# One order of steps replaced by another in a hand-scheduled kernel of block-sparse attention, Fourier mixing and an MLP

## The chip, the cores and the metric

The kernel runs on one core of a Trainium2 chip. The metric is the device time of one execution in microseconds (us). A core has five engines that work beside each other, each through its own list of instructions in order: TensorE (PE in the profile; its weight loads are PEld), VectorE (DVE), ScalarE (ACT), GpSimd (POOL) and SyncE (SP), which here only issues DMAs. An instruction whose input or whose buffer isn't ready makes its engine wait, and all that stands behind it in that engine's list waits too.

## The reference

Queries, keys and values have 4 batches, 8 heads, 768 positions and 64 channels. Keys are averaged over blocks of 64 positions; each query keeps its own block and those among the 3 best of the 12 blocks by a gate score, and attends causally within them. The heads are put side by side into `x` (768 x 512 a batch), which is mixed by a two-dimensional Fourier transform and sent through an MLP with a residual:

```python
    k_rep = k.reshape(B, H, n_blocks, block, D).mean(axis=3)
    gate_scores = np.einsum('bhsd,bhnd->bhsn', q, k_rep)
...
    top_idx = np.argsort(gate_scores, axis=-1)[..., -top_k:]
...
    mask = mask & (pos[:, None] >= pos[None, :])
    scores = np.where(mask, scores, -1000000000.0)
...
    return np.matmul(attn, v).astype(np.float32)
...
    X = np.fft.fft(x, axis=1)
    X = np.fft.fft(X, axis=2)
    mixed = np.real(X).astype(np.float32)
    u = x + mixed
    mu = np.mean(u, axis=-1, keepdims=True)
    var = np.mean((u - mu) ** 2, axis=-1, keepdims=True)
    un = (u - mu) / np.sqrt(var + 1e-06)
    ch = np.maximum(un @ w_ch1, 0.0) @ w_ch2
    return (u + ch).astype(np.float32)
```

## The kernel before

The work is cut into 16 pairs of heads, P = 0 to 15, four to a batch b. Every piece of work is a step with a short name and its indices, and the string `ORDER` lists all steps of the program in one sequence. A loop at the end of the kernel calls them in that sequence (lines 765 to 769), inside a context that leaves the instructions of each engine in the order in which they were called. So the string fixes five lists, one for each engine. What an engine waits for follows from the data: the framework adds a wait wherever an instruction reads what another engine writes, overwrites what another still reads, or shares a PSUM tile with another engine.

The steps, in the order in which a pair and then a batch passes through them:

- Loads, issued by SP: `Lq`, `Lk`, `Lv` (lines 263 to 283). `Li` loads a constant. `W` and `X` load the weights of the MLP, issued by POOL.
- Preparing a pair: `tk`, `tq` turn keys and queries on PE in early pairs; later pairs are turned on VectorE by `kb` and `qc`. `ks`, `kh` make block sums on VectorE, `kc` copies the keys on ScalarE, `qs` copies the queries on POOL.
- The gate: `g` on PE, then `gt`, `gx`, `gl`, `gm` on VectorE; from pair 7 on, `K` writes the mask into the query buffer with eight copies on POOL (line 400).
- Scores: `s:P,i` on PE, six tiles i = 0 to 5 (line 410), `e:P,i` the exponential on ScalarE, `d:P,i` the causal select on POOL for the part on the diagonal. `vc` converts the values on POOL. `v` multiplies the exponentials of a pair with its values (42 matmuls, PE), and needs all six `d` and `vc`; `x` divides by the sums on VectorE.
- Fourier transform of a batch: `fs`, `fd`, `f` fold `x` by symmetry on VectorE. `pg` is a small read on POOL that stands ahead of the reuse of a buffer. `y:b,0` and `y:b,1` are the first transform on PE, `ty` (ScalarE) and `tr` (VectorE) copy its result in two ways, `m:b,0` to `m:b,2` are the second transform on PE.
- Sum and normalization: `u` (VectorE) adds `x`, `xu` (ScalarE) scales the sum, and `un` turns it for the MLP, for batch 0 on PE and VectorE (`xt`, `un`), for batches 1 to 3 by two DMA transposes on SP for each `un` (line 605). `bn`, `nv` (VectorE) and `nr` (POOL) make the reciprocal deviation.
- MLP: `w:b,it`, it = 0 to 15, is the first product, 8 matmuls on PE that need all three `un` of the batch; `r` is its relu, on ScalarE, for every fourth on VectorE. `c:b,st,h` is the half h of the second product for the 128 rows st, 8 matmuls; two neighbouring st share one PSUM tile. `o` scales and adds the residual on VectorE, `od` stores the rows (SP). In the last batch the rows st = 5 are cut into two halves of the columns instead, each with 16 matmuls (`c:3,5,0` and `c:3,5,1`, `o:3,5` and `o:3,6`).

All PSUM tiles of the kernel come from one pool of four tiles of two banks each: score tiles, gate tiles, `v`, `y`, `m`, `w` and `c` share them. A `c` tile is held from its first half product until both of its `o`. The exponentials have two buffers, so the first `e` of a pair needs the `v` of an earlier one to be done; `u` has five buffers, so some `u` need a store of an earlier batch to have landed.

Of the kernel before, what the change touches and what calls it, by code (L numbers as in the profile page):

```python
# [173 lines left out]
r:3,11 nv:3 c:3,5,0 c:3,5,1 c:3,0,0 nr:3 pg:3 c:3,1,0 c:3,0,1 c:3,1,1 o:3,0 c:3,2,0 c:3,2,1 o:3,5
c:3,4,0 c:3,4,1 o:3,6 c:3,3,0 o:3,1 o:3,2 o:3,4 c:3,3,1 o:3,3 od:3,1 od:3,5 od:2,5 od:2,2 od:3,0
od:2,4 od:2,3 od:3,2 od:3,6 od:3,4 od:3,3
"""
assert PT_W == 5376 and len(COL) == 42

# [620 lines left out]
```

## Time and profile before

| | us |
|---|---|
| median of 3 executions | 294.94 |
| lowest and highest | 294.92 and 302.59 |
| the profiled execution | 294.79 |
| its span, from first to last instruction | 292.8 |

The span is the profile's own time and lies 2.0 us below the device time of that execution. In the profile, L668 is a line of the source, and an operand pair such as `c<-w_sb,hT` names the tile written and the tiles read. The lines that matter here: `sc` L421 and L426 are the steps `s`, `pt` L443 `e`, `pt` L449 `d`, `av` L461 `v`, `yp` L531 and L537 `y`, `mx` L564 and L565 `m`, `u` L578 `u`, `x` L590 `xu`, `h` L641 and L643 `w`, `hT` L651 and L653 `r`, `c` L660 and L668 `c`, `u` L680 `o`. L221 and L224 are helpers that many steps on VectorE and POOL share.

A matmul's own duration contains the time that it takes to run through the pipeline, in which the next one already runs. What a step costs TensorE is therefore read from a run of many of its matmuls, not from the duration of one.

### The profile page before, as it was taken

To read this page: it belongs to the slowest core of one execution; us is meant where nothing else is said; L and a number is where in the kernel's file an instruction comes from. 1 tells how busy PE (TensorE), PEld (TensorE's weight loads), DVE (VectorE), ACT (ScalarE), POOL (GpSimd) and SP (SyncE) were. 2 spreads that over 40 slices of the span, in tenths; PEclk is the share of its full clock that TensorE was granted. 3 is DMA by queue.
4 is the path that set the end of the run, shared out by engine and by line. 5 is a ranking of instruction groups with operands and counts; after the bars stand their busy time and mean duration, and the time that the engine had idled before them with its cause. 6 is when DMAs were issued, how large, how long until landed. Compare 5 with 4: busy or idle time off the path is not lost.

```text
span 292.8 us, 6583 instructions
## 1 busy us (share of the span) xinstructions
PE 276.4 (94%) x2537; PEld 169.1 (58%) x2537; DVE 198.3 (68%) x604; ACT 164.1 (56%) x205; POOL 113.2 (39%) x286
## 2 busy tenths in 40 slices
PE   7799999899999999989999999999999998999993
PEld 4466777655556456635665466556655644657441
DVE  2999999989875998969758858862672457212022
ACT  3698989866686437579858463776242240534000
POOL 2267527406689598400790483438000000003000
PEclk9999999999999999999999999999999999999999
DMA  9999999999999968376700021930000332000063
GB/s 201 268 222 238 198 206 196 202 175 161 158 209 167 192 126 171 66 144 178 112 2 1 0 85 42 128 108 0 2 2 0 143 67 44 0 2 0 2 233 125
DMA packets 118287, 33.52 MB, mean 114 GB/s; under 512 B 111024, under 2 KB 115056, under 8 KB 118256
## 3 DMA queue, kind: packets, MB, share of 16 engines
q1 hardware_dynamic: 112592, 28.47, 45.6%
q0 software_dynamic: 3664, 4.19, 9.0%
q10 hardware_dynamic: 2000, 0.44, 0.7%
q8 instruction: 20, 0.33, 0.5%
q14 instruction: 11, 0.09, 0.1%
HBM read 28.63 MB, written 6.29 MB: 119 GB/s over the span
## 4 chain that ended last, share of the span: by engine, by line
PE 63%; DVE 16%; ACT 8%; SPq 6%; DMA 3%; issue 2%; POOL 0%; DVEq 0%; ACTq 0%; POOLq 0%
PE c L668 21%; PE h L641 15%; PE h L643 8%; ACT pt L443 5%; SPq L277 5%; PE sc L426 5%; PE av L461 4%; DVE kr L306 2%; PE yp L531 2%; DVE u L680 2%; DVE q L328 2%; DMA nat<-in_q_dram 1%; PE warmps L705 1%; DVE u L578 1%; PE c L660 1%
## 5 line engine op out<-in xcount | busy, mean ns | idle before, releaser
L443 ACT ACTIVATE pt<-sc 128x1024 f16<-128x1024 f32 (+1 forms) x96 | 83.0, 923 | 27.6 <-PE sc L426 22.9
L668 PE MATMUL c<-w_sb,hT 128*128 128x512 f16 x368 | 83.8, 379 | 2.6 <-DVE u L680 2.6
L641 PE MATMUL h<-unT,w 128*128 128x512 f16 x256 | 84.7, 380 | 0.6 <-DVE unT L602 0.2
L643 PE MATMUL h<-unT,w 128*128 128x256 f16 x256 | 69.8, 273 | 0.0
L653 ACT ACTIVATE hT<-h 128x768 f16<-128x768 f32 x48 | 37.4, 809 | 42.9 <-PE h L643 42.7
L668 PEld LDWEIGHTS <-hT 128*128 128x128 f16 x368 | 35.4, 98 | 42.0 <-issue 3.3
L449 POOL TENSOR_SCALAR_AFFINE_SELECT pt<-pt 128x256 f16<-128x256 f16 x96 | 37.2, 413 | 48.8 <-ACT pt L443 32.5
L641 PEld LDWEIGHTS <-w 128*128 128x128 f16 x256 | 25.0, 98 | 29.6 <-issue 0.9
L680 DVE SCALAR_TENSOR_TENSOR u<-c,rs,u 128x512 f32<-128x512 f32 (+1 forms) x25 | 17.3, 720 | 35.3 <-PE c L668 31.8
L224 POOL TENSOR_SCALAR_AFFINE_SELECT qk<-mt 32x160 f16<-32x160 f16 x72 | 23.6, 348 | 16.5 <-DVE mt L398 14.9
L643 PEld LDWEIGHTS <-w 128*128 128x128 f16 x256 | 25.0, 98 | 5.3 <-issue 1.4
L426 PE MATMUL sc<-qk 96*128 96x128 f16 (+3 forms) x144 | 26.8, 306 | 1.2 <-ACT pt L443 1.2
L221 POOL TENSOR_TENSOR t<-vr,rs 128x6 f32<-128x6 f32 x12 | 2.4, 198 | 63.8 <-DVE rs L621 63.2
L651 DVE TENSOR_SCALAR hT<-h 128x768 f16<-128x768 f32 x16 | 15.1, 951 | 17.3 <-PE h L643 17.1
L224 POOL TENSOR_SCALAR_AFFINE_SELECT qk<-q 64x768 f16<-64x768 f32 (+1 forms) x25 | 20.8, 831 | 15.5 <-DVE q L328 11.0
L461 PE MATMUL av<-v,pt 128*128 128x65 f16 x672 | 23.1, 194 | 1.0 <-DVE u L578 1.0
L461 PEld LDWEIGHTS <-pt 128*128 128x128 f16 x672 | 22.2, 97 | 3.2 <-POOL qk L224 0.8
L590 ACT ACTIVATE x<-u,nm 128x512 f16<-128x512 f32 x24 | 15.8, 715 | 12.6 <-DVE nm L584 12.3
L426 PEld LDWEIGHTS <-qk 96*128 96x128 f16 x144 | 13.1, 98 | 10.7 <-issue 1.6
L578 DVE SCALAR_TENSOR_TENSOR u<-mx,x 128x512 f32<-128x512 f32 x24 | 15.6, 685 | 4.3 <-PE mx L565 2.5
L610 DVE BATCH_NORM_STATS2 bst<-u 128x6 f32<-128x512 f32 x24 | 16.1, 670 | 0.0
L421 PE MATMUL sc<-qk 64*128 64x512 f16 (+3 forms) x112 | 14.6, 306 | 1.5 <-ACT pt L443 0.8
(99 smaller groups left out, 353.4 us busy)
## 6 DMA issues: line engine op xcount, KB each, us to landing
nat<-in_v_dram SPq DMA_DIRECT2D x16, 384.0 KB, 5.0
out_dram<-u SPq DMA_DIRECT2D x23, 256.0 KB, 2.3
nat<-in_q_dram SPq DMA_DIRECT2D x36, 96.0 KB, 3.0
nat<-in_k_dram SPq DMA_DIRECT2D x17, 192.0 KB, 3.6
nat<-in_k_dram SPq DMA_DIRECT2D x28, 96.0 KB, 2.9
nat<-in_q_dram SPq DMA_DIRECT2D x13, 192.0 KB, 3.6
w_sb<-in_moe_w_ch_dram POOLq DMA_DIRECT2D x2, 1024.0 KB, 10.0
w<-in_moe_w_ch_dram POOLq DMA_DIRECT2D x2, 768.0 KB, 9.3
```

What stands on the lines that cost most here:

```text
L224: nc.gpsimd.affine_select(out=out, in_=in_, pattern=[[0, i] for i in n], base=0, channel_multiplier=0, compare_op=ALU.is_ge, fill=0.0)
L426: nc.tensor.matmul(ps[:, e, co:co + q1 - q0], qk[0:96, e, 1, 128 * jt:128 * jt + 128], qk[0:96, e, 0, q0:q1], start=True, stop=True)
L443: nc.scalar.activation(out=d["pt"][:, o:o + 2 * n].rearrange("p (e c) -> p e c", e=2), in_=d["sc", i][:, :, 0:n], func=AF.Exp, scale=0.125)
L449: nc.gpsimd.affine_select(out=dg, in_=dg, pattern=[[0, 2], [1, 128]], base=0, channel_multiplier=-1, compare_op=ALU.is_ge, fill=0.0)
L461: nc.tensor.matmul(av[:, e, 66 * st:66 * st + 65], pt[:, co:co + 128], vv[:, e, jt, 0:65], start=(cnt == 0), stop=(cnt == 20))
L578: nc.vector.scalar_tensor_tensor(out=u_b[:, k2, :].rearrange("p (m two) -> p two m", two=2), in0=mps[:, k2, :].rearrange("p (two m) -> p t ...
L610: nc.vector.bn_stats(out=bst, in_=u_t[b, kt // 2][:, kt % 2, :])
L641: nc.tensor.matmul(hp[:, 0:512], w1s, unT[:, dt, 0:512], start=(dt == 0), stop=(dt == NDT - 1))
L643: nc.tensor.matmul(hp[:, 512:768], w1s, unT[:, dt, 512:768], start=(dt == 0), stop=(dt == NDT - 1))
L653: nc.scalar.activation(out=hT, in_=hp, func=AF.Relu)
L668: nc.tensor.matmul(c_ps[b, g[0]][:, st - g[0], :], h_t[b, it][:, 128 * st:128 * (st + 1)], w2_sb[:, it, :], start=(it == 0), stop=(it == N ...
L680: nc.vector.scalar_tensor_tensor(out=o, in0=ps, scalar=st_t[b][1][:, st:st + 1], in1=o, op0=ALU.mult, op1=ALU.add)
```

## The change

The string `ORDER` is the same up to `w:0,4` in the middle of the first MLP product of batch 0, and another one from there to its end. Both hold the same steps, each once; nothing else in the kernel differs. Each PSUM tile's reads and writes stand in the string in an order that every engine keeps. These lines are the first of the diff and the last:

```diff
-r:0,12 w:0,7 r:0,7 s:6,5 s:6,2 w:0,13 r:0,13 e:6,5 w:0,10 w:0,4 w:0,3 e:6,2 qc:10 gx:8 kb:10 ks:10
-kh:10 qc:9 d:6,1 d:6,4 d:6,0 qs:7 K:7 vc:5 d:6,2 X:0 d:5,3 Li:0 Lv:7 Lq:12 Lv:8 Lv:9 s:7,5 r:0,3
...
-r:3,11 nv:3 c:3,5,0 c:3,5,1 c:3,0,0 nr:3 pg:3 c:3,1,0 c:3,0,1 c:3,1,1 o:3,0 c:3,2,0 c:3,2,1 o:3,5
-c:3,4,0 c:3,4,1 o:3,6 c:3,3,0 o:3,1 o:3,2 o:3,4 c:3,3,1 o:3,3 od:3,1 od:3,5 od:2,5 od:2,2 od:3,0
+r:0,12 w:0,7 r:0,7 s:6,5 s:6,2 w:0,13 r:0,13 e:6,5 w:0,10 w:0,4 d:5,3 vc:5 qs:7 d:6,4 K:7 X:0 Li:0
+Lv:7 Lq:12 Lv:8 Lv:9 qc:9 gx:8 gl:8,0 gl:8,1 gm:8 kb:10 kh:9 bn:0,5 v:5 s:7,5 e:6,2 g:9 gt:9 s:7,0
...
+pg:3 nr:3 r:3,13 w:3,15 r:3,15 c:3,5,1 c:3,4,1 c:3,0,0 c:3,2,1 o:3,4 o:3,6 c:3,0,1 o:3,2 o:3,0
+c:3,3,1 o:3,3 c:3,1,0 c:3,1,1 c:3,5,0 o:3,1 o:3,5 od:3,6 od:2,3 od:2,2 od:2,4 od:3,4 od:3,2 od:3,0
```

Read for single engines, the parts of the two lists that the prediction speaks of are these. TensorE, from the parting to the first MLP product of batch 1, old and new:

```
old: w:0,3 s:7,5 v:5 s:7,0 w:0,14 g:9 g:10 w:0,8 s:7,4 w:0,15 s:7,3 s:7,1 w:0,11 s:7,2 w:0,9 v:6
     s:8,4 s:8,3 c:0,2,0 c:0,3,0 s:8,1 v:7 c:0,0,0 s:8,0 s:9,2 c:0,1,0 s:9,4 c:0,3,1 s:8,5 c:0,1,1
     s:9,3 s:9,5 c:0,2,1 c:0,0,1 y:1,1 g:11 y:1,0 s:9,0 s:8,2 c:0,4,0 s:9,1 m:1,1 m:1,0 m:1,2 v:8
     v:9 c:0,5,0 c:0,5,1 s:11,5 s:11,1 s:10,1 c:0,4,1 s:10,0 g:12 s:11,0 s:10,4 s:11,3 w:1,1
new: v:5 s:7,5 g:9 s:7,0 s:7,3 w:0,8 s:7,4 w:0,3 s:7,1 s:7,2 s:8,3 w:0,9 w:0,14 w:0,11 v:6 s:8,5
     w:0,15 g:10 c:0,0,0 s:9,1 v:7 s:8,4 c:0,1,0 s:8,2 c:0,2,0 s:8,1 s:8,0 c:0,0,1 s:9,5 c:0,1,1
     y:1,1 y:1,0 c:0,3,0 m:1,0 m:1,1 c:0,4,0 s:9,3 c:0,3,1 s:9,4 s:9,0 c:0,2,1 m:1,2 c:0,5,0 g:11
     c:0,5,1 s:9,2 v:8 s:10,5 c:0,4,1 s:10,3 s:10,0 v:9 s:10,2 s:11,0 w:1,0
```

TensorE, from the second transform of batch 2, and of batch 3, to the first `w` of the batch:

```
old: m:2,2 m:2,0 m:2,1 c:1,4,1 v:12 c:1,2,0 c:1,5,1 s:14,3 c:1,3,0 s:14,0 s:14,4 v:13 s:15,3 c:1,3,1
     s:15,0 s:14,5 s:15,5 c:1,2,1 s:14,2 w:2,3
new: m:2,0 c:1,5,1 s:15,1 s:15,4 m:2,1 s:15,0 v:13 c:1,2,0 s:14,4 m:2,2 c:1,2,1 s:14,5 s:14,1 s:14,2
     c:1,3,0 c:1,3,1 s:15,5 s:14,0 s:15,2 w:2,4
old: m:3,1 m:3,0 c:2,5,0 m:3,2 c:2,2,0 c:2,2,1 c:2,4,1 c:2,5,1 c:2,3,0 c:2,3,1 w:3,15
new: m:3,1 m:3,0 c:2,0,0 c:2,1,0 w:2,10 c:2,4,0 c:2,1,1 c:2,0,1 c:2,4,1 c:2,2,0 c:2,3,0 m:3,2 c:2,5,0
     c:2,2,1 c:2,3,1 c:2,5,1 w:3,14
```

POOL from the parting on, and SP around the transposes:

```
POOL old: d:6,1 d:6,4 d:6,0 qs:7 K:7 vc:5 d:6,2 X:0 d:5,3 d:7,5 d:7,0 vc:6 vc:7 K:8 qs:9 d:6,5 d:6,3
          d:7,4 X:1 d:7,1 d:7,2 d:7,3 vc:8 K:9 vc:9 nr:0
POOL new: d:5,3 vc:5 qs:7 d:6,4 K:7 X:0 qs:9 K:8 d:7,3 d:6,3 d:6,2 d:6,5 d:6,0 d:7,4 vc:6 d:7,2 d:6,1
          d:7,5 X:1 qs:10 K:9 vc:7 d:7,0 d:7,1 nr:0
SP old:   Lq:13 od:0,1 Lq:14 od:0,2 od:0,0 Lk:12 Lk:13 un:1,1 un:1,0 un:1,2 Lk:14
SP new:   Lq:13 od:0,1 od:0,0 Lq:14 Lk:12 un:1,1 un:1,2 un:1,0 od:0,3 Lk:13 Lk:14
SP old:   od:1,1 od:1,0 Lv:14 un:2,2 Lv:15 un:2,1 un:2,0 od:1,3 od:1,5 od:2,0 od:1,2 od:2,1 od:1,4
          un:3,0 un:3,2 un:3,1
SP new:   Lv:14 Lv:15 od:1,1 od:1,0 un:2,1 un:2,0 un:2,2 od:1,3 od:1,2 od:1,5 od:1,4 un:3,1 un:3,0
          od:2,1 od:2,0 un:3,2
```

VectorE around the sums of batch 1, and at the end:

```
old: tr:1,0 qc:12 gx:11 gl:11,0 gl:11,1 gm:11 u:1,1 u:1,0 u:1,2 x:8 kb:12 x:9
new: tr:1,0 u:1,1 gl:10,0 u:1,0 bn:1,3 gl:10,1 kb:11 ks:11 kh:11 gm:10 qc:12 o:0,2 u:1,2 gt:11 gx:11
     o:0,3 gl:11,0 bn:1,0 gl:11,1 gm:11 x:8
old: u:3,0 u:3,1 u:3,2 bn:3,2 o:2,5 o:2,2 ... o:3,0 o:3,5 o:3,6 o:3,1 o:3,2 o:3,4 o:3,3
new: u:3,1 o:2,0 o:2,1 bn:3,2 bn:3,3 u:3,2 o:2,4 o:2,2 ... o:3,4 o:3,6 o:3,2 o:3,0 o:3,3 o:3,1 o:3,5
```

More of the change, by code (lines that the diff above doesn't have):

```diff
@@ new lines @@
+fs:7,1 fd:7,1 fs:4,0 fd:6,0 qc:11 fd:7,0 fd:6,1 f:1,1 f:1,0 f:1,2 f:1,3 y:1,1 e:9,1 e:8,4 e:8,2
+e:8,1 e:8,0 e:9,5 o:0,0 o:0,1 ty:1,1 y:1,0 c:0,3,0 tr:1,1 ty:1,0 m:1,0 tr:1,0 m:1,1 c:0,4,0 s:9,3
+c:0,3,1 s:9,4 s:9,0 c:0,2,1 e:9,3 u:1,1 gl:10,0 m:1,2 xu:1,1 e:9,0 c:0,5,0 u:1,0 bn:1,3 Lv:10 Lv:11
+Lk:11 Lq:13 od:0,1 od:0,0 Lq:14 Lk:12 gl:10,1 kb:11 ks:11 kh:11 gm:10 qc:12 g:11 c:0,5,1 o:0,2 e:9,4
+kc:10 u:1,2 kc:11 xu:1,2 gt:11 gx:11 s:9,2 o:0,3 gl:11,0 xu:1,0 e:9,2 bn:1,0 gl:11,1 gm:11 d:8,2
+vc:8 vc:9 d:8,3 d:8,1 d:8,4 d:9,5 qs:11 d:8,5 d:9,1 d:9,3 d:9,4 d:8,0 d:9,0 vc:10 K:10 qs:12 d:9,2
@@ new lines @@
+pg:1 K:11 vc:11 v:8 s:10,5 c:0,4,1 s:10,3 s:10,0 x:8 o:0,4 o:0,5 kb:12 ks:12 kh:12 v:9 s:10,2 s:11,0
+un:1,1 un:1,2 un:1,0 od:0,3 Lk:13 Lk:14 od:0,5 Lv:12 od:0,4 Lv:13 Lk:15 Lq:15 od:0,2 w:1,0 x:9 g:12
+s:11,2 s:11,4 e:10,5 s:10,4 w:1,12 e:10,3 gt:12 e:10,0 w:1,10 s:11,1 e:10,2 e:11,0 s:11,5 w:1,1
+r:1,0 e:11,2 s:10,1 kb:13 ks:13 gx:12 gl:12,0 fs:9,1 gl:12,1 gm:12 kb:14 qc:13 kh:13 fs:9,0 fs:8,0
+w:1,8 e:10,4 e:11,4 w:1,11 r:1,12 r:1,11 r:1,10 e:11,5 r:1,1 s:11,3 e:10,1 w:1,6 qc:14 ks:14 kh:14
@@ new lines @@
+w:1,15 w:1,13 r:1,8 kc:13 g:14 e:11,3 g:13 e:11,1 r:1,15 gt:13 r:1,6 gx:13 bn:1,4 gl:13,0 gl:13,1
+w:1,5 gm:13 d:11,5 d:10,5 d:10,1 d:10,4 d:10,2 d:11,4 K:12 d:11,3 d:10,3 d:11,2 d:11,0 d:10,0 K:13
+d:11,1 qs:13 qs:14 v:10 gt:14 w:1,4 r:1,5 gx:14 x:10 gl:14,0 fs:10,0 bn:1,1 w:1,2 w:1,7 r:1,4 kc:12
+v:11 r:1,7 r:1,13 x:11 fs:11,0 qc:15 r:1,2 w:1,3 r:1,3 s:12,0 kc:14 e:12,0 s:13,3 w:1,9 s:12,4
+s:13,5 w:1,14 s:13,2 e:13,3 r:1,9 e:13,5 c:1,0,0 gl:14,1 gm:14 kb:15 fs:10,1 bn:1,5 ks:15 kh:15
+r:1,14 e:12,4 s:12,2 g:15 bn:1,2 nv:1 gt:15 s:12,5 c:1,1,0 s:13,4 e:13,2 s:12,1 e:12,2 e:12,1
@@ new lines @@
+c:1,0,1 s:12,3 e:12,5 e:13,4 s:13,0 e:12,3 s:13,1 kc:15 e:13,1 c:1,1,1 c:1,4,0 e:13,0 gx:15 fs:8,1
+fs:11,1 fd:11,1 gl:15,0 fd:10,0 fd:11,0 fd:10,1 f:2,1 f:2,2 gl:15,1 gm:15 f:2,0 f:2,3 nr:1 d:12,0
+d:12,1 d:13,3 d:13,2 d:13,5 d:12,3 qs:15 d:12,5 d:12,4 d:12,2 vc:12 d:13,0 K:15 K:14 pg:2 d:13,1
+d:13,4 vc:13 y:2,0 v:12 c:1,4,1 ty:2,0 y:2,1 o:1,0 s:15,3 tr:2,0 c:1,5,0 ty:2,1 m:2,0 c:1,5,1 o:1,1
+x:12 s:15,1 s:15,4 fs:12,0 tr:2,1 e:15,3 m:2,1 e:15,1 s:15,0 e:15,4 v:13 u:2,0 xu:2,0 c:1,2,0 o:1,4
+s:14,4 o:1,5 m:2,2 u:2,1 xu:2,1 c:1,2,1 x:13 s:14,5 bn:2,3 e:15,0 e:14,4 u:2,2 fs:13,1 fs:13,0
@@ new lines @@
+bn:2,1 s:14,1 s:14,2 c:1,3,0 c:1,3,1 bn:2,0 bn:2,4 bn:2,5 bn:2,2 nv:2 e:14,5 o:1,2 s:15,5 o:1,3
+xu:2,2 Lv:14 Lv:15 od:1,1 od:1,0 un:2,1 un:2,0 un:2,2 od:1,3 od:1,2 od:1,5 od:1,4 s:14,0 e:14,1
+e:14,2 e:15,5 e:14,0 s:15,2 w:2,4 r:2,4 e:15,2 s:14,3 w:2,8 r:2,8 w:2,7 e:14,3 w:2,3 r:2,3 r:2,7
+w:2,14 d:14,4 d:15,0 d:14,2 d:14,5 d:15,4 d:15,3 nr:2 d:15,2 d:15,5 d:15,1 vc:15 d:14,3 d:14,1
+d:14,0 vc:14 v:15 w:2,13 w:2,11 r:2,13 v:14 r:2,11 w:2,6 r:2,14 w:2,0 w:2,9 w:2,2 w:2,5 r:2,9 r:2,2
+r:2,0 r:2,5 x:15 w:2,1 x:14 r:2,1 fs:14,0 fs:15,0 fs:15,1 fs:12,1 fd:15,1 fs:14,1 fd:14,0 fd:14,1
@@ new lines @@
+fd:15,0 f:3,2 f:3,1 f:3,3 f:3,0 y:3,1 ty:3,1 y:3,0 tr:3,0 r:2,6 w:2,15 ty:3,0 w:2,12 r:2,12 tr:3,1
+m:3,1 m:3,0 c:2,0,0 u:3,0 c:2,1,0 w:2,10 r:2,15 c:2,4,0 r:2,10 c:2,1,1 c:2,0,1 u:3,1 c:2,4,1 c:2,2,0
+c:2,3,0 o:2,0 m:3,2 o:2,1 c:2,5,0 bn:3,2 bn:3,3 u:3,2 c:2,2,1 xu:3,1 xu:3,0 xu:3,2 un:3,1 un:3,0
+od:2,1 od:2,0 un:3,2 o:2,4 c:2,3,1 c:2,5,1 o:2,2 bn:3,0 w:3,14 w:3,0 w:3,1 r:3,0 w:3,3 r:3,14 w:3,12
+bn:3,5 o:2,3 r:3,12 w:3,7 w:3,4 bn:3,1 w:3,5 r:3,5 w:3,2 r:3,3 r:3,1 w:3,6 r:3,6 w:3,11 r:3,2 r:3,4
@@ L177 @@
+w:3,10 o:2,5 r:3,7 w:3,9 r:3,9 c:3,2,0 c:3,3,0 w:3,8 c:3,4,0 r:3,8 r:3,10 r:3,11 w:3,13 bn:3,4 nv:3
+pg:3 nr:3 r:3,13 w:3,15 r:3,15 c:3,5,1 c:3,4,1 c:3,0,0 c:3,2,1 o:3,4 o:3,6 c:3,0,1 o:3,2 o:3,0
+c:3,3,1 o:3,3 c:3,1,0 c:3,1,1 c:3,5,0 o:3,1 o:3,5 od:3,6 od:2,3 od:2,2 od:2,4 od:3,4 od:3,2 od:3,0
+od:3,3 od:2,5 od:3,1 od:3,5
 """
```

46 lines of the change are left out of this document (5 added, 41 removed).

## The prediction

> **What bounds the kernel now.** First the head of the page and its busy time by engine.
>
> ```profile
> span 292.8 us, 6583 instructions
> ## 1 busy us (share of the span) xinstructions
> PE 276.4 (94%) x2537; PEld 169.1 (58%) x2537; DVE 198.3 (68%) x604; ACT 164.1 (56%) x205; POOL 113.2 (39%) x286
> ```
>
> TensorE is the candidate. A mean over the span doesn't say where it stands idle, so next I read the busy time by stretch, from the point at which the two lists part. The first two columns are the stretch and its length, then come busy time and instructions of PE, PEld, DVE, ACT and POOL, then the granted clock.
>
> ```profile
> 74.60:115.00 40.40, 39.69 (x362) 23.88 (x360) 32.79 (x105) 24.68 (x30) 32.76 (x73) 1.00 0.98 172
> 115.00:130.00 15.00, 12.57 (x148) 7.69 (x146) 12.52 (x34) 9.17 (x13) 5.34 (x15) 1.00 0.54 96
> 130.00:230.00 100.00, 99.85 (x837) 60.92 (x835) 66.60 (x193) 59.57 (x74) 37.45 (x103) 1.00 0.27 58
> 230.00:245.00 15.00, 13.44 (x73) 6.97 (x73) 8.81 (x25) 4.00 (x6) 0.00 (x0) 1.00 0.36 89
> 245.00:285.00 40.00, 40.00 (x234) 22.78 (x233) 9.97 (x19) 9.07 (x12) 2.50 (x13) 1.00 0.11 42
> 285.00:292.80 7.80, 2.95 (x13) 1.07 (x11) 2.16 (x3) 0.00 (x0) 0.00 (x0) 0.95 0.34 124
> 206.60:218.30 11.70, 11.70 (x78) 7.04 (x75) 7.98 (x17) 3.24 (x4) 0.00 (x0) 1.00 0.01 1
> ```
>
> PE is full from 130 to 230 and from 245 to 285, at clock 1.00. Where it isn't full, it misses 40.40 - 39.69 = 0.71, 2.43, 0.15 and 1.56 us in the first, second, third and fourth stretch. Of the 4.85 us in the sixth, part is a stall and the rest is the time behind the last product. The PE timeline of two of these stretches names the stalls (in brackets: idle time, and who ended it).
>
> ```profile
> 117.06 1.44 PE L461 MATMUL av<-v,pt 128*128 128x65 f16 x42 [0.52 <-DVE u L578]
> 119.03 1.45 PE L461 MATMUL av<-v,pt 128*128 128x65 f16 x42 [0.52 <-DVE u L578]
> ```
>
> ```profile
> 242.62 3.62 PE L668 MATMUL c<-w_sb,hT 128*128 128x512 f16 x16 [1.50 <-DVE u L680]
> ```
>
> Last the timeline of all engines at the end.
>
> ```profile
> 286.10 1.41 DVE L680 SCALAR_TENSOR_TENSOR u<-c,rs,u 128x512 f32<-128x512 f32 x2 [6.34 <-PE c L668]
> 286.88 3.06 SPq L685 DMA_DIRECT2D out_dram<-u  x4
> 286.90 1.89 PE L668 MATMUL c<-w_sb,hT 128*128 128x512 f16 x8 [0.84 <-DVE u L680]
> ```
>
> PE ends at 286.90 + 1.89 = 288.79; the last result step and store take the other 4.01 us. So behind the cut TensorE has 0.71 + 2.43 + 0.15 + 1.56 + 0.84 = 5.69 us of stalls. The change adds and removes no instruction, so PE's work is the same before and after. The time moves by two things alone: the sum of these stalls, and what lies behind PE's last product. That caps the gain at 5.7 us and what the end gives; the loss has no such cap.
>
> **The prices.** From the chain of waits, which cuts TensorE's stream into pieces without overlap:
>
> ```profile
> 71.98 0.38 PE h L641
> ...
> 159.78 3.45 PE c L668 x16
> 163.24 0.86 PE sc L426 x4
> ...
> 187.07 1.28 PE av L461 x42
> ```
>
> Half a column sum `c` (8 matmuls) is 1.73 us, a score tile `s` 0.43 (the small tile `s:P,5` about 0.1, an estimate by its columns), a pair's `v` 1.28. The last row of the table by stretch holds nine whole products `w` in 11.70 us: 1.30 each. `w:0,10` starts at 71.98 and `w:0,4` is the last step that both lists share on PE, so the new order begins there at about 71.98 + 2 x 1.30 = 74.6. `m` has half the columns of a half `c`: 0.87, an estimate.
>
> For the other engines, the groups of POOL, VectorE and ScalarE (count | busy, mean ns of one | idle before):
>
> ```profile
> L449 POOL TENSOR_SCALAR_AFFINE_SELECT pt<-pt 128x256 f16<-128x256 f16 x96 | 37.2, 413 | 48.8 <-ACT pt L443 32.5 <-issue 9.0 <-PE c L668 6.7
> L224 POOL TENSOR_SCALAR_AFFINE_SELECT qk<-mt 32x160 f16<-32x160 f16 x72 | 23.6, 348 | 16.5 <-DVE mt L398 14.9
> L224 POOL TENSOR_SCALAR_AFFINE_SELECT qk<-q 64x768 f16<-64x768 f32 x18 | 15.0, 833 | 4.5 <-DVE q L326 3.2 <-PE sc L426 0.7
> L224 POOL TENSOR_SCALAR_AFFINE_SELECT v<-nat 128x768 f16<-128x768 f32 x16 | 14.5, 914 | 0.2
> ```
>
> ```profile
> L680 DVE SCALAR_TENSOR_TENSOR u<-c,rs,u 128x512 f32<-128x512 f32 x23 | 16.6, 742 | 35.3 <-PE c L668 31.8 <-POOL rs L221 3.5
> L610 DVE BATCH_NORM_STATS2 bst<-u 128x6 f32<-128x512 f32 x24 | 16.1, 670 | 0.0
> L578 DVE SCALAR_TENSOR_TENSOR u<-mx,x 128x512 f32<-128x512 f32 x24 | 15.6, 685 | 4.3 <-PE mx L565 2.5 <-DMA out_dram<-u 1.7
> ...
> L326 DVE STREAM_TRANSPOSE q<-nat 128x768 f32<-128x768 f32 x9 | 8.7, 967 | 0.0
> ```
>
> ```profile
> L590 ACT ACTIVATE x<-u,nm 128x512 f16<-128x512 f32 x24 | 15.8, 715 | 12.6 <-DVE nm L584 12.3
> ```
>
> And the transposes that SP issues (line 605), and the stores:
>
> ```profile
> L605 SPq DMA_TRANSPOSE unT<-x x18: 1189/1220/2121, 118.5 to 242.5; - x18
> ...
> DMA to landing us min/median/max: 2.4/2.5/5.2
> ```
>
> ```profile
> out_dram<-u SPq DMA_DIRECT2D x23, 256.0 KB, 2.3
> ...
> out_dram<-u SPq DMA_DIRECT2D x2, 128.0 KB, 2.0
> ```
>
> **The change part by part.** *POOL's new order up to the first `v`.* POOL now takes `d:5,3`, `vc:5` and `qs:7` first, whose inputs are long there, and defers the selects of pair 6. From `K:7` to the last step that `v:7` needs, `d:7,1`, its list holds three `K` of about 8 x 0.348 + 0.3 = 3.1, two `qs` of 1.7, two `vc` of 0.91, eleven `d` at about 0.4 and two weight loads that I take at 0.9 each: 9.3 + 3.4 + 1.8 + 4.4 + 1.8 = 20.7 us. `K:7` waits for a VectorE step that isn't moved and starts near 70.5, so `v:7` can start near 91.2. On PE there stand ahead of `v:7`, from 74.6: `v:5`, `v:6` (2.6), seven full and two small `s` (3.2), `g:9`, `g:10` (0.9, an estimate), six `w` (7.8), one `c` (1.7): 16.2, that is 90.8. Stall about 0.4 (0 to 1.5), where the old order misses 0.71 in its stretch.
>
> *First chain (batch 1, where 2.43 us are lost now).* The new list does three halves `c` fewer before `y:1,1` and keeps them for the chain. Behind `m:1,1` PE has, up to `w:1,0`: six halves `c` (10.4), `m:1,2` (0.9), eight full and one small `s` (3.5), two `v` (2.6), `g:11` (0.4): 17.8. The chain meanwhile needs `u:1,1` and `u:1,0` (2 x 0.685 and a short step, 1.5 each), then on VectorE what stands ahead of `u:1,2`: `bn` (0.9 with its second instruction), `kb:11`, `ks:11`, `qc:12` (about 0.97 each), `o:0,2` (0.74) and short steps (0.6), 5.1 together; `u:1,2` 1.5; `xu:1,2` 2 x 0.715 = 1.4; two transposes for `un:1,2` (2.4), one more (1.2) and the landing of the last (2.5): 17.1. Cover and need are even. I take 0.5 for handovers; the bounds are 0 and, with the slowest landing of 5.2, about 2.5.
>
> *Second chain (batch 2, nearly hidden now).* The new list places `m:2,2` late. Behind it stand three halves `c` (5.2), four full and two small `s` (1.9): 7.1. Need: `u:2,2` 1.5, `xu:2,2` 1.4, a transpose 1.2, landing 2.5: 6.6. Again even: 0.5 (0 to 2.5), where the old order loses at most 0.15.
>
> *Third chain (batch 3, 1.56 lost now).* In the old order `o:2,5` stands ahead of `o:2,2` on VectorE and waits for `c:2,5,1`, and PE's `c:2,3,0` waits for `o:2,2`: the 1.50 of the row. The new order finishes `c:2,3,0` before any `o` of that tile, so this stall goes. What is late next is `un:3,2`: behind `m:3,2` only four halves `c` are left (6.9) against 1.5 + 1.4 + 1.2 + 2.5 = 6.6. I take 0.5 (0 to 2.5).
>
> *The end.* Now `o:3,2` waits 6.34 us for PE although its half of the tile was summed long before, and `c:3,3,1`, which writes the other half, waits 0.84 for `o:3,2`. In the new list another half `c` stands between each `o` and the next access to its tile (1.73 against 0.74), so the 0.84 goes. The last product is the half-width `c:3,5,0`, its `o` about 0.37 (half of 0.742, an estimate) instead of 0.742, its store 2.0 instead of 2.3: 0.67 less behind PE's end.
>
> The Trainium skill, PSUM — Partial Sum Buffer, section PSUM bank collisions raise a hardware error, asks that engines be kept apart by bank and quadrant only; the two halves of this tile are two banks, so by it `c:3,3,1` need not have waited. The trace differs: the program does wait, 0.84 us, so it orders whole tiles. By the page the end would give 0.67 alone and the sum would come out 0.8 us higher, near 291.9.
>
> *Sum.* Stalls of 5.69 go; 0.4 + 0.5 + 0.5 + 0.5 come, and 0.6 for the tight places that I costed at nothing (PSUM tiles freed less than 0.5 us ahead of their next use, in the second score phase above all; cover: the running product of 1.30). That is 2.5, so 3.2 less stall and 0.67 less end: 3.9 us. The profiled execution takes 294.79 for a span of 292.8, the median is 294.94, so they stand 0.15 apart: 290.9 for the one, **291.1 us** for the median.
>
> **Rivals.** *Nothing is left of the stalls.* All chains are even in my sums, so a little luck hides them: 294.94 - 5.69 - 0.67 = 288.6, just over 2% faster. For it: 100 us at 99.85 in the old order show that it can be done. Against: four even races must all be won. Chance 0.10.
>
> *The stalls only move.* Each of the four even races is lost by about 1 us more: 291.1 + 4 = 295, no change. For it: the 0.52 and 0.52 on `u` and the 1.50 show that each chain cost something before. Chance 0.14.
>
> *The transposes land late.* In the new SP list a load of queries, two stores and two more loads stand right ahead of `un:1,1`, two loads and two stores ahead of `un:2,1`, and two stores between `un:3,0` and `un:3,2`. If the last transpose of each batch lands after 5.2 instead of 2.5, three even chains lose 2.7 each: 291.1 + 8.1 = 299.2, slower than before; it decides from 1.3 us late on in each. For it: 5.2 did happen. Against: the median is 2.5 beside the minimum of 2.4, and the old list has two loads of keys ahead of its first transposes. Chance 0.16, half of it, with other in-order blocks on POOL and VectorE, above 2% slower.
>
> The Trainium skill, TensorE: Matmul & The Clock Gate, section What's actually happening, says that an idle window of about 3.4 us halves the PE clock. No stretch above shows that: stalls stay at 1.50 us or less and the clock at 1.00. By the page a single stall of that length would make this rival dearer by some 2 us.
>
> That the list doesn't do what it says is hardly open: both hold the same steps.
>
> **Numbers.** The forecast, 289.1 to 293.5, has 0.60. With the chances above the range is **288.7 to 298.0**: below it lies about 0.06, above it about 0.11. Two per cent, about what a measurement of this kernel can tell from no change, is 5.9 us. Faster by more needs under 289.0: 0.10. Slower by more needs over 300.8: 0.08. Within: 0.82.
>
> **What would show it.** In the new profile: PE idle behind 74.6 near 2.5 us, with stalls at `v:7` (released by POOL), and before the first `w` of batches 1, 2 and 3 (released by the transposes), none on `u` of line 680; PE's stretch ahead of `y:1,1` some 5 us shorter; under 3.6 us behind PE's last matmul. The prediction is wrong if PE's busy time itself differs, if waits on PSUM tiles (ACT or DVE releasing `sc` or `h`) add up to over 2 us, or if a store or load blocks the transposes.

## The result and the profile after

| | before | after |
|---|---|---|
| median, us | 294.94 (294.92 to 302.59) | 292.99 (292.94 to 293.06) |
| the profiled execution, us | 294.79 | 292.97 |
| its span, us | 292.8 | 291.2 |

The ratio is 0.9934, interval 0.9915 to 0.9954: 1.95 us faster, or 0.7%, where 3.84 were forecast. Some executions, such as the one at 302.59, are disturbed: the ratios and the medians of the runs below leave them out, and the profiles of `b_o22`, `b_tail` and `b_u`, which are of such executions, are read only for single stalls and for the clock.

First the page of the new order: span, instructions and busy time of the engines.

```profile
span 291.2 us, 6585 instructions
## 1 busy us (share of the span) xinstructions
PE 276.6 (95%) x2537; PEld 169.2 (58%) x2537; DVE 202.9 (70%) x604; ACT 163.6 (56%) x205; POOL 116.1 (40%) x286
```

TensorE has its 2537 matmuls in the same busy time, as the prediction demands. But VectorE is busy 4.6 us longer (198.3 before) and POOL 2.9 us longer (113.2 before), with 604 and 286 instructions in both. The same instructions in another order take longer. That is the first sign of what the forecast lacked.

Next the busy time by the stretches of the prediction (length, then PE, PEld, DVE, ACT, POOL, then the granted clock).

```profile
74.60:115.00 40.40, 38.27 (x350) 23.28 (x349) 34.15 (x95) 21.52 (x27) 26.36 (x59) 1.00 0.92 163
115.00:130.00 15.00, 14.92 (x163) 8.45 (x162) 13.56 (x40) 13.06 (x17) 10.15 (x25) 1.00 0.38 81
130.00:230.00 100.00, 98.02 (x831) 60.53 (x830) 70.23 (x203) 59.66 (x76) 40.37 (x104) 1.00 0.27 63
230.00:245.00 15.00, 15.00 (x75) 7.24 (x74) 5.93 (x14) 2.42 (x4) 0.00 (x0) 1.00 0.44 89
245.00:285.00 40.00, 40.00 (x227) 22.00 (x226) 12.15 (x23) 9.18 (x12) 2.40 (x12) 1.00 0.15 54
```

PE misses 40.40 - 38.27 = 2.13 us in the first stretch (0.71 before), 0.08 in the second (2.43), 1.98 in the third (0.15), nothing in the fourth (1.56) and fifth. The old holes are closed, and new ones have opened in the stretches that were nearly full. The list of PE's waits behind 72 us names them (releaser, then total, number and longest in us).

```profile
PE h L641 <- DVE hT L651: 1.1, 1, 1.1
PE av L461 <- POOL v L224: 0.6, 1, 0.6
PE yp L531 <- DVE fg L513: 0.5, 1, 0.5
PE yp L531 <- DVE fg L516: 0.5, 1, 0.5
PE c L668 <- ACT hT L653: 0.5, 1, 0.5
PE h L641 <- ACT hT L653: 0.4, 1, 0.4
PE h L641 <- ACT pt L443: 0.3, 1, 0.3
```

In the order of time these are 1.11 before `w:0,15` (at 88.40, VectorE's relu of a `w` tile late), 0.53 and 0.48 before and inside `y:1,1` (at 103.12 and 104.29, VectorE's fold late), 0.35 before `w:1,15`, 0.43 before `w:1,14`, 0.47 before `c:1,0,0` (at 159.32) and 0.61 before `v:12` (at 173.48, POOL late). With two of about 0.1 and gaps under 0.05 the sum is 4.19. No product `w` waits for a transpose for longer than 0.08.

Last the timeline of the end, all engines.

```profile
285.59 1.91 PE L660 MATMUL c<-w_sb,hT 128*128 128x256 f16 x16
285.79 0.75 DVE L680 SCALAR_TENSOR_TENSOR u<-c,rs,u 128x512 f32<-128x512 f32 x1 [2.70 <-PE c L668]
286.57 1.81 SPq L685 DMA_DIRECT2D out_dram<-u  x2
287.54 0.48 DVE L680 SCALAR_TENSOR_TENSOR u<-c,rs,u 128x256 f32<-128x256 f32 x1 [1.00 <-PE c L660]
```

PE ends at 287.50. Behind it lie 3.70 us, not under 3.6: the last `o` takes 0.48 instead of 0.75, but from its end (288.02) to the end of the span it is 3.2, as before, where the last `o` ended at 288.83 + 0.75 = 289.58 and the span at 292.8:

```profile
288.83 0.75 DVE L680 SCALAR_TENSOR_TENSOR u<-c,rs,u 128x512 f32<-128x512 f32 x1 [1.32 <-PE c L668]
```

Behind 74.6 TensorE is without a product for 5.70 + 4.01 us before and 4.19 + 3.70 after, 1.82 less. The spans are only 1.6 apart, because its busy time there is 0.2 us longer (208.49 before, 208.71 after, for the same matmuls). That the device times of the profiled executions also stand 1.82 apart is chance: the device time lies 2.0 us above the span before and 1.8 after.

### The profile page after: what moved, and what is told of

Read it like the earlier page. It is cut to its first block, busy times and chain, and to the rows that moved or that the text cites. A ratio compares the mean times of both kernels' runs of the same rounds, so it can differ in the third digit from the quotient of the medians.

```text
span 291.2 us, 6585 instructions
## 1 busy us (share of the span) xinstructions
PE 276.6 (95%) x2537; PEld 169.2 (58%) x2537; DVE 202.9 (70%) x604; ACT 163.6 (56%) x205; POOL 116.1 (40%) x286
## 3 DMA queue, kind: packets, MB, share of 16 engines
q0 software_dynamic: 3664, 4.19, 8.8%
## 4 chain that ended last, share of the span: by engine, by line
PE 68%; DVE 17%; ACT 8%; POOL 4%; issue 2%; DVEq 0%; ACTq 0%; POOLq 0%
PE c L668 24%; PE h L641 15%; PE h L643 7%; ACT pt L443 5%; PE sc L426 5%; PE av L461 4%; DVE kr L306 2%; PE yp L531 2%; PE mx L564 2%; POOL pt L449 2%; DVE q L328 2%; PE mx L565 2%; DVE mx L378 1%; PE warmps L705 1%; DVE u L578 1%
## 5 line engine op out<-in xcount | busy, mean ns | idle before, releaser
L449 POOL TENSOR_SCALAR_AFFINE_SELECT pt<-pt 128x256 f16<-128x256 f16 x96 | 40.0, 444 | 49.1 <-ACT pt L443 48.6
L651 DVE TENSOR_SCALAR hT<-h 128x768 f16<-128x768 f32 x16 | 15.1, 948 | 27.3 <-PE h L643 27.3
L224 POOL TENSOR_SCALAR_AFFINE_SELECT qk<-q 64x768 f16<-64x768 f32 (+1 forms) x25 | 21.5, 862 | 15.0 <-DVE q L328 11.0
L426 PE MATMUL sc<-qk 96*128 96x512 f16 (+3 forms) x144 | 26.2, 306 | 0.0
L221 POOL TENSOR_TENSOR t<-vr,rs 128x6 f32<-128x6 f32 x12 | 2.9, 242 | 54.5 <-DVE rs L621 53.8
```

The costliest lines, as they stand in the source:

```text
L224: nc.gpsimd.affine_select(out=out, in_=in_, pattern=[[0, i] for i in n], base=0, channel_multiplier=0, compare_op=ALU.is_ge, fill=0.0)
L426: nc.tensor.matmul(ps[:, e, co:co + q1 - q0], qk[0:96, e, 1, 128 * jt:128 * jt + 128], qk[0:96, e, 0, q0:q1], start=True, stop=True)
L449: nc.gpsimd.affine_select(out=dg, in_=dg, pattern=[[0, 2], [1, 128]], base=0, channel_multiplier=-1, compare_op=ALU.is_ge, fill=0.0)
```

## The experiments

**Two local changes alone, in the old order.** The first swaps two neighbours, `o:2,2` ahead of `o:2,5`; the second only takes the new order of the last steps, from the column sums of batch 3 on.

```diff
-c:2,4,1 c:2,5,1 bn:3,2 o:2,5 o:2,2 c:2,3,0 c:2,3,1
+c:2,4,1 c:2,5,1 bn:3,2 o:2,2 o:2,5 c:2,3,0 c:2,3,1
```

> The old order with one swap on VectorE: `o:2,2` ahead of `o:2,5`. If the 1.50 us stall before `c:2,3,0` comes from that order alone, it goes, and the next limit is the last transpose of batch 3 (second issue at 242.5, landing 2.5 later, 245.0, while `w:3,15` started at 246.07): a gain of 1.1 us, to 293.8, with some 0.4 us of new stall before `w:3,15`. Rival, that the transposes already set the start of `w:3,15`: a gain of 0.2 at most, 294.7 to 294.9, with 1.5 us of stall before `w:3,15` instead.

```diff
-nv:3 c:3,5,0 c:3,5,1 c:3,0,0 nr:3 pg:3 c:3,1,0 c:3,0,1 c:3,1,1 o:3,0 c:3,2,0 c:3,2,1 o:3,5
-c:3,4,0 c:3,4,1 o:3,6 c:3,3,0 o:3,1 o:3,2 o:3,4 c:3,3,1 o:3,3 ...
+nv:3 c:3,2,0 c:3,3,0 c:3,4,0 pg:3 nr:3 c:3,5,1 c:3,4,1 c:3,0,0 c:3,2,1 o:3,4 o:3,6 c:3,0,1 o:3,2
+o:3,0 c:3,3,1 o:3,3 c:3,1,0 c:3,1,1 c:3,5,0 o:3,1 o:3,5 ...
```

> The old order up to `nv:3`, then the steps that are left in the order that the new list gives them. If the end of the new list is worth what its trace shows (the 0.84 us stall gone, 0.3 us less behind the last matmul): 1.1 us less, 293.8. Rival, that the eleven stores that are queued at the end set it: 0.2 at most, 294.7, with PE's end earlier and more time behind it.

The first took 293.29 (ratio 0.9924, interval 0.9869 to 0.998), the second 293.44 (0.9945, 0.9928 to 0.9963); by the medians they gained 1.6 and 1.5 us where 1.1 were expected, and the first interval is wide. PE's waits on the line of `o`, first run, then second (the source lines stand three higher):

```profile
PE c L665 <- DVE u L677: 1.1, 2, 0.8
```

```profile
PE c L665 <- DVE u L677: 1.7, 2, 1.5
```

In the one trace the 1.50 is gone, in the other the 0.84. Behind the 1.50 a wait of 0.31 for the last transpose of batch 3 came up, near the 0.4 expected. Both terms were real and could be had without the rest of the change.

**The stall of 1.11.** Why is VectorE late at 88 us? The VectorE timeline of the new order shows `fs:5,1` (L221), the three instructions of `nv:0` (L617 to L621), and then the relu (L651) for which PE waits:

```profile
84.35 1.02 DVE L221 TENSOR_TENSOR sd<-x 128x384 f16<-128x384 f16 x1
85.29 0.79 DVE L617 TENSOR_SCALAR vr<-mv 128x6 f32<-128x6 f32 x1
86.11 0.17 DVE L619 TENSOR_SCALAR rs<-vr 128x6 int32<-128x6 int32 x1
86.32 0.68 DVE L621 TENSOR_SCALAR rs<-rs 128x6 int32<-128x6 int32 x1
...
87.42 0.92 DVE L651 TENSOR_SCALAR hT<-h 128x768 f16<-128x768 f32 x1
```

Six numbers a partition take 0.79 and 0.68 us, where L619 of the same size takes 0.17. POOL beside it copies the queries of pair 10 (`qs:10`, two instructions behind the weight load):

```profile
84.24 0.89 POOL L739 DMA_DIRECT2D w_sb<-in_moe_w_ch_dram  x1
85.14 1.83 POOL L224 TENSOR_SCALAR_AFFINE_SELECT qk<-q 64x768 f16<-64x768 f32 x2
```

L621 ends at 87.00, `qs:10` at 86.97; L617 ends at 86.08, about where the first of the two copies must end (half of 1.83 behind 85.14 is 86.05). So the suspicion was that VectorE's instruction waits for POOL's to finish, with the wait inside its own duration. Against it stood the simpler reading, that `nv:0` merely stands in the way. One kernel moves `nv:0` (and `nr:0`, which needs it) behind the relus, the other leaves VectorE's list alone and moves only `qs:10`.

```diff
-fs:5,1 nv:0 gl:9,1 ... d:7,0 d:7,1 nr:0 kc:9 ... r:0,11 kh:10 w:0,15
+fs:5,1 gl:9,1 ... d:7,0 d:7,1 kc:9 ... r:0,11 kh:10 nv:0 nr:0 w:0,15
```

> The new order with `nv:0` (and `nr:0` behind it in the string) moved behind `r:0,11` and `kh:10` on VectorE. Both theories of the 1.11 us stall before `w:0,15`, that VectorE's list there is too long and that `nv:0` and `fs:5,1` were stretched by POOL work beside them, expect the stall to fall to 0.2 or less and the time to about 291.9. Rival: the next wait (`v:7` behind POOL's `d:7,1`) takes the place, 292.6 to 293.0. By the second theory `nv:0` itself falls from 1.7 us to about 0.5 to 0.9 where no POOL instruction lies beside it.

```diff
-X:1 qs:10 K:9 vc:7 d:7,0 d:7,1 nr:0
+X:1 K:9 vc:7 d:7,0 d:7,1 qs:10 nr:0
```

> The new order, VectorE's list untouched, with POOL's two copies `qs:10` moved from ahead of `K:9` to behind `d:7,1`. If instructions of `nv:0` wait for the POOL copy that runs beside them, `nv:0` falls from 1.71 us to about 0.6, `r:0,11` starts about 1 us earlier and the stall before `w:0,15` falls from 1.11 to about 0.1 to 0.4: 292.0 to 292.3. If VectorE's list alone is too long there, `nv:0` stays at 1.7 us, the stall stays at 1.1 and so does the time, 293.0.

Without `nv:0` in the way: 292.22 (0.9905, 0.9887 to 0.9923), the stall at 0.11; the three instructions of `nv:0`, now beside other work of POOL, take 0.16, 0.20 and 0.26. Both readings expect the stall to go there. With `qs:10` moved, where they differ: 291.73 (0.989, 0.9874 to 0.9905), the stall gone. VectorE in that trace (the source lines stand two lower), then POOL beside it:

```profile
83.95 0.35 DVE L219 TENSOR_TENSOR sd<-x 128x384 f16<-128x384 f16 x1
84.22 0.48 DVE L615 TENSOR_SCALAR vr<-mv 128x6 f32<-128x6 f32 x1
84.74 0.38 DVE L617 TENSOR_SCALAR rs<-vr 128x6 int32<-128x6 int32 x1
85.15 0.17 DVE L619 TENSOR_SCALAR rs<-rs 128x6 int32<-128x6 int32 x1
```

```profile
83.84 0.89 POOL L737 DMA_DIRECT2D w_sb<-in_moe_w_ch_dram  x1
84.78 0.30 POOL L402 MEMSET qk<- 32x256 f16 x1
```

`fs:5,1` takes 0.35 instead of 1.02 although nothing of VectorE's list was touched. `nv:0` fell from 1.71 to 1.10 only, not to the 0.6 expected, and what is left follows the same rule: its first instruction ends at 84.70 beside a POOL instruction that ends at 84.73, its second at 85.12 beside one that ends at 85.08. From the start of `fs:5,1` to the end of `nv:0` it is now 1.37 us instead of 2.65. The cause of the 1.11 is shown: a POOL copy put beside VectorE's chain. Of the moves of single steps this is the only one whose interval lies clear of that of the new order (0.9915 to 0.9954); for the others the stalls in the traces carry the reading.

**The stalls of `y:1,1`.** They wait for the last two folds, `f:1,2` and `f:1,3`; the edit makes these first.

```diff
-fd:6,1 f:1,1 f:1,0 f:1,2 f:1,3 y:1,1
+fd:6,1 f:1,2 f:1,3 f:1,1 f:1,0 y:1,1
```

> The new order with `f:1,2` and `f:1,3`, which `y:1,1` needs, ahead of `f:1,1` and `f:1,0` on VectorE. If the stalls of 0.53 and 0.48 us before and in `y:1,1` come from the order of the four folds: `y:1,1` starts at once, `y:1,0` may then wait some 0.5 us for `f:1,0`, a gain of 0.5 to 1.0, 292.0 to 292.5. Rival, that the end of the four folds, stretched by POOL's work beside them, sets the start of `y:1,0` in any order: under 0.3, 292.7 to 293.0.

292.32 (0.9911, 0.989 to 0.9931): both stalls gone, and 0.67 come back before `y:1,0`, which needs `f:1,0`. The order of four steps was worth about a third of the 1.01 in stalls. In this trace the copy in `f:1,0` (L506), now the last of the four, takes 0.80 us and ends 0.04 behind a POOL copy of queries (`qs:11`), the part of the rival that held; moving `qs:11` is tried below.

**The stall of `v:12`.** On POOL the queries of pair 15 stand ahead of the conversion that `v:12` needs.

```diff
-d:12,3 qs:15 d:12,5 d:12,4 d:12,2 vc:12 d:13,0
+d:12,3 d:12,5 d:12,4 d:12,2 vc:12 qs:15 d:13,0
```

> The new order with POOL's `qs:15` moved from ahead of `d:12,5` to behind `vc:12`. If the 0.61 us stall before `v:12` is the length of POOL's list ahead of `vc:12`: it goes, 292.4. A second effect: the copy in `f:2,3`, 0.80 us beside `qs:15`, becomes shorter, 0.4 or less. Rival: PE then waits as long for the folds of batch 2 or for `qs:15` at `s:15,3`: 292.9.

292.65 (0.9921, 0.9896 to 0.9947), the stall gone; the gain of 0.34 in the median is inside the spread. The second effect came as expected: the copy in `f:2,3` takes 0.38 instead of 0.80.

**The stalls of 0.43 and 0.47.** The copy of the keys of pair 14 on ScalarE runs ahead of both; it was moved far behind.

```diff
-s:12,0 kc:14 e:12,0 ... e:13,1 c:1,1,1 c:1,4,0 e:13,0 gx:15
+s:12,0 e:12,0 ... e:13,1 c:1,1,1 c:1,4,0 e:13,0 kc:14 gx:15
```

> The new order with ScalarE's `kc:14` (1.68 us, first needed some 30 us later) moved from ahead of `e:12,0` to behind `e:13,0`. If the stalls of 0.43 and 0.47 us before `w:1,14` and `c:1,0,0` come from ScalarE's backlog: they go, 292.1. Rival, that they come from the few PSUM tiles whoever frees them: they stay within 0.3 us, 292.7 to 293.0.

293.01 (0.9927, 0.9904 to 0.9951): no gain, and both stalls stay at 0.43 and 0.46. A miss. This copy on ScalarE isn't what they wait for; what is left as reading is the turn of the PSUM tiles (the releaser is each time the step that frees one), which this run doesn't show by itself. The trace has something else: the last copy of batch 1's folds takes 0.38 instead of 0.80 without any edit near it, because `qs:11` begins later and a select runs beside it, and the 0.48 inside `y:1,1` is 0.07. So what stands beside what can change from one execution to the next.

**All four together**, and then with `kc:13` later and `e:12,4` ahead of `r:1,14` besides:

> The new order with the four moves together: `qs:10` behind `d:7,1`, the folds of batch 1 in the other order, `qs:15` behind `vc:12`, `kc:14` behind `e:13,0`. If each stall is worth its own length: 292.99 - 1.26 (measured for `qs:10`) - 0.5 to 1.0 - 0.6 - 0.9 = 289.2 to 289.7. Rival, that a stall taken away turns up at the next tight place: half of it, 291.

```diff
-r:1,8 kc:13 g:14 e:11,3 g:13 e:11,1 r:1,15 ... ks:15 kh:15 r:1,14 e:12,4 s:12,2
+r:1,8 g:14 e:11,3 g:13 e:11,1 kc:13 r:1,15 ... ks:15 kh:15 e:12,4 r:1,14 s:12,2
```

> The new order with the four moves and two more on ScalarE: `kc:13` behind `e:11,1`, and `e:12,4` ahead of `r:1,14`. Moving `kc:14` left the stalls of 0.43 and 0.47 us, so what sets them is which PSUM tile is freed when. If so, `c:1,0,0` gets the tile of `e:12,4` instead of that of `r:1,14` (0.47 less) and `w:1,15` the tile of `e:11,3` 1.7 us earlier (0.35 less): 290.41 - 0.8 = 289.6. Rival, that ScalarE's total is the limit there and the waits move to the next tile: 290.2 to 290.4.

290.41 (0.9848, 0.9824 to 0.9872) with 1.84 us of stalls left, and 290.17 (0.9845, 0.9827 to 0.9862) with 2.05. The first lies between its two forecasts: 2.58 us under the new order, near the sum of what the moves gave alone (1.26 + 0.67 + 0.34), without the 0.9 that `kc:14` was to bring. In the second the 0.47 before `c:1,0,0` and the 0.35 before `w:1,15` went, as the turn of the tiles has it, but 0.40 before `g:14` came and the wait before the second half of `y:1,0` grew from 0.32 to 0.88: the time is that of the rival. At this last the same sight as at 86 us: VectorE's short copy in `f:1,0`, then POOL.

```profile
101.89 0.80 DVE L506 COPY fg<-zw 128x6 f16<-128x6 f16 x1
```

```profile
101.44 2.10 POOL L224 TENSOR_SCALAR_AFFINE_SELECT qk<-q 64x768 f16<-64x768 f32 x2
```

**The suspicion tried a second time.** Only POOL's `qs:11` moves, by two selects.

```diff
-d:8,4 d:9,5 qs:11 d:8,5 d:9,1 d:9,3
+d:8,4 d:9,5 d:8,5 d:9,1 qs:11 d:9,3
```

> The second version of all moves (290.17) with the copy of queries `qs:11` on POOL two selects later, so that it doesn't run beside the short copy L506 of `f:1,0` on VectorE, which took 0.80 us there and holds `y:1,0`'s second half for 0.88. If POOL's instruction is what stretches the copy: L506 at 0.4 or less, the stall of 0.88 at 0.1 to 0.4, time 289.5 to 289.9. If the copy is slow for another reason: 0.80 and 0.88 stay, time 290.2. If the wait only moves (v:8 or y:1,0's next reader late): the stall goes and another of about 0.5 comes, time 290.2.

VectorE and POOL at that place:

```profile
102.08 0.38 DVE L506 COPY fg<-zw 128x6 f16<-128x6 f16 x1
```

```profile
98.78 4.00 POOL L449 TENSOR_SCALAR_AFFINE_SELECT pt<-pt 128x256 f16<-128x256 f16 x6
102.74 1.70 POOL L224 TENSOR_SCALAR_AFFINE_SELECT qk<-q 64x768 f16<-64x768 f32 x2
```

The copy takes 0.38, the stall fell to 0.45, the time is 289.75 (289.15 to 291.48; 0.9845, 0.9809 to 0.9881). POOL's two copies are shorter as well, 1.70 instead of 2.10: the loss was on both sides. Of PE's waits three are left in the list, 0.45 of them still on the fold:

```profile
PE yp L531 <- DVE fg L507: 0.4, 1, 0.4
PE h L641 <- ACT hT L653: 0.4, 1, 0.4
PE g L354 <- ACT hT L653: 0.4, 1, 0.4
```

This has the lowest median of all kernels here; from the two before it the intervals don't part it.

**The old order with both local changes.**

> The old order with both single changes: `o:2,2` ahead of `o:2,5`, and the end of the new list. The two were worth 1.1 to 2 us and 1.4 to 1.6 us alone and lie in different batches. If what the new list gains is these late stalls and the first chain's, less the new ones in between: 294.9 - 1.2 - 1.4 = 292.3, which is below the new order's 292.99 although the first chain's 2.4 us stay. Rival, that the two overlap (stores of batch 2 queue at the end): 293.2 to 293.5.

291.86 (0.9903, 0.9883 to 0.9923), 3.1 us by the median, about the sum of the two. Two local changes in the old list beat the whole new one by 1.1 us in the median (the intervals touch at their ends), though they leave the first chain as it was:

```profile
PE sc L426 <- ACT pt L443: 1.2, 1, 1.2
PE av L461 <- DVE u L578: 1.1, 2, 0.5
```

**The first chain of the old order.** The sums `u` of batch 1 were put ahead of `qc:12` and the gate of pair 11 on VectorE.

```diff
-Lk:13 qc:12 gx:11 gl:11,0 gl:11,1 gm:11 u:1,1 e:9,1 m:1,0 u:1,0 m:1,2 kc:11 ... K:11 u:1,2 v:8
+Lk:13 u:1,1 e:9,1 m:1,0 u:1,0 m:1,2 u:1,2 qc:12 gx:11 gl:11,0 gl:11,1 gm:11 kc:11 ... K:11 v:8
```

> The old order with its two swaps (291.86), and the sums `u:1,1 u:1,0 u:1,2` on VectorE ahead of `qc:12` and the gate of pair 11 instead of behind them (nothing else moves). If the PSUM tiles of `m`, held until their `u`, are what costs the old order its first chain: the two stalls of 0.54 and 0.53 in front of `v:8` and `v:9` go, time 290.8 to 291.2. Rival, the gate that is now later holds `K:11` and the scores of pair 11, where a stall of 1.17 stands already: the 1.17 grows by about what the others lose, time 291.6 to 292.4.

A miss on both times: 295.69 (1.0056, 1.0028 to 1.0084), slower than the old order and some 4.5 us slower by the ratios than the list it started from (0.9903). The two stalls before `v:8` and `v:9` are gone, as the first theory has it. The rival had the right place, `K:11` and the scores of pair 11, but not the size: the copy of the queries of pair 12 now waits for the late `qc:12`, POOL stands still for 4.28 and writes the mask of pair 11 behind it, and PE gets a new stall (POOL's timeline, then PE's):

```profile
125.03 1.71 POOL L224 TENSOR_SCALAR_AFFINE_SELECT qk<-q 64x768 f16<-64x768 f32 x2 [4.28 <-DVE q L326]
```

```profile
129.72 1.00 PE L426 MATMUL sc<-qk 96*128 96x128 f16 x6 [2.31 <-POOL qk L224]
131.89 1.01 PE L426 MATMUL sc<-qk 96*128 96x256 f16 x4 [1.17 <-ACT pt L443]
132.98 3.57 PE L668 MATMUL c<-w_sb,hT 128*128 128x512 f16 x8
```

The stall is 2.31 with the 1.17 unchanged behind it, and behind both eight matmuls take 3.57 us, where the same take 1.89 in the timelines before. What that is stands in the last section. The other long stall in this trace, 3.44 at `v:6`, is no part of the edit: POOL, which `v:6` waits for, had stood 4.92 us behind a load of values.

## Why the forecast was half right

The time, 292.99, lies in the range of 288.7 to 298.0 and in the narrower 289.1 to 293.5, but the gain is half of what was forecast. Term by term:

*PE's time is fixed, stalls and end decide*: right, to the 0.2 us of busy time above.

*The old stalls go*: right, all of them. The 1.50 and the 0.84 went by local changes alone, as `b_o22` and `b_tail` show, and nothing waits on `u` of line 680. The reading that waits go by whole tiles, which the prediction sets against the page on PSUM of the Trainium skill, fits: the 0.84 vanished when another half `c` came between.

*0.4 before `v:7`*: it was 0. Both sides came later than summed: POOL's `d:7,1` ended at 92.27 instead of 91.2 and TensorE reached `v:7` at 92.37 instead of 90.8, 1.11 of it by the stall ahead. Without that stall, in `a_nv0`, `v:7` begins at 91.58 and runs through though `d:7,1` ends at 91.88. So a `v` can begin before the last of its `d` is done, other than the list of the steps says; in the trace of `b_u`, too, `v:6` runs 15 products before it waits.

*Three even races at 0.5 each*: all three won, with 0.08 us in all. The bound below, 0, was the right end, and narrowly: the last transposes landed at 127.72, 195.81 and 245.08, and the first `w` of the batches began at 127.96, 195.91 and 245.78. Cover and need were even as the sums had them; that all three fell on the good side is luck, as the prediction itself says of four.

*0.6 for the tight places that I costed at nothing*: this is the step that failed. They cost 4.1 us: 1.11 + 0.53 + 0.48 + 0.35 + 0.11 + 0.43 + 0.47 + 0.61. Of these 1.11 + 0.35 + 0.43 + 0.47 = 2.36 are waits for a PSUM tile that ScalarE or VectorE frees, over the 2 us that the prediction gave as a sign of being wrong. The folds (1.01) and `v:12` (0.61) stood in no term. The two places on VectorE's side, 1.11 and 1.01, lie up to `y:1,1`, in the stretch where I had followed POOL only; `y:1,1` still began at 103.12 instead of 107.44, 4.3 us earlier where about 5 were forecast. The sizes came from the old trace, in which each instruction stands beside its old neighbours. For the 1.11, `a_qs10` shows the cause, for the copy of `f:1,0` `a_all3` does. For the 0.61 it is an in-order block on POOL (`a_vc12`). For the 0.35, 0.43 and 0.47 it stays open in part: the 0.35 and the 0.47 go with two other moves on ScalarE (`a_all2`), none goes with `kc:14`, and the turn of the PSUM tiles is argued, not shown.

*0.67 at the end*: 0.31 by the rounded spans, all of it from the last `o`, which gave 0.27, not 0.37. The other 0.3, a shorter way for a half store, didn't come: 3.2 us from the last `o` to the end both times. The 2.0 us were the median landing of two stores of 128 KB; in the new profile the same group takes 2.7. In the traces of `a_qs10`, `b_tail` and `b_both`, with the same last steps, it is 2.9 from the last `o` to the end; why it isn't so in the others is not settled.

The sum: 3.87 forecast, less 4.19 - 2.5 = 1.69 for the stalls, less 0.67 - 0.31 = 0.36 for the end, leaves the 1.82 that TensorE stands less without a product. The 1.69 is the difference of two larger errors: 1.9 us of stalls were forecast at `v:7` and at the races and 0.08 came, 0.6 were forecast for the tight places and 4.1 came. That the first makes up for half of the second is luck.

*The rivals.* Nothing left of the stalls: no, 4.19, though the new order with seven moves (`a_all3`) comes within 1.2 us of that rival's 288.6. The stalls only move: 4.2 of the 5.7 us are there again, but not at the places named. The transposes land late: no.

## What to carry to other kernels

Before a list is reordered as a whole, look for the one or two places where steps stand in each other's way: a swap of two neighbours and another order of the last steps gave 3.1 us here, the whole new list 1.95. When steps are moved, an instruction's duration isn't a constant that moves with it: write down beside which instruction of the other engine it will stand, VectorE beside POOL above all, and put POOL's long copies where VectorE has no one waiting. A step costed at nothing needs its cover written out as the others do; the sum of such steps was the largest term.
